# Dynamic convolution with a gated two-stage network: row-half streams from the second head on, eight unsplit experts in the second stage, no join, every task's place written out

## The chip, the cores and the metric

The kernel runs on one core of a Trainium2 chip. A core has TensorE (PE in the rows; PEld is its weight load), VectorE (DVE), ScalarE (ACT), GpSimd (POOL) and SyncE (SP, which here only issues DMAs). They run at the same time, each through its own instructions in order, and wait for each other by semaphores. The metric is the device time of one execution in microseconds (us). TensorE's granted clock was 1.000 over the whole span, the upper of its two levels.

## The reference, cut to what matters

```python
# stage 1: x (4, 4160, 192), weight_gen (4, 4160, 8, 7)
w = softmax(weight_gen, axis=-1)                    # 7 taps for each token and head
out[b, s, h, g] = sum_k w[b, s, h, k] * x_pad[b, s + k, h, g]     # 6 zeros ahead of x
# stage 2: w_in (192, 1024), conv_w (3, 1024), w_out (1024, 192)
h = maximum(out @ w_in, 0)
conv = sum_k conv_w[k] * h_pad[:, k:k + S]          # over 3 neighbouring tokens
y = (h * sigmoid(conv)) @ w_out                     # (4, 4160, 192), float32
```

## The kernel before, in words

The 16,640 tokens lie on 128 partitions, 130 on each. A block `j` is 4 of these (512 tokens); there are 33 blocks. The 1024 hidden columns are 8 groups of 128, which the change's title calls experts (`f`). The work of a block is:

- **Head** `q`: POOL multiplies x by seven taps into `px` and `py` (for the first two heads VectorE takes some). For heads 0 to 2 TensorE sums the seven products while it transposes them; from head 3 on two accumulating DMAs and two POOL adds sum them first, so that only 6 transposes are left. ScalarE (`split_hi`) and VectorE (`split_lo`) write the transposed tile as a rounded part and a rest: `H1` and `L1` for the first 128 columns of x, `H2` for the last 64, with the rounded part in rows 0 to 63 and the rest in rows 64 to 127.
- **First stage**, `unit(j, f)`: matmuls of `wi` with `H1`, `H2`, `L1` into one of five PSUM banks `z`; ScalarE writes `relu` into `h` and the middle tap of the convolution back into `z`; VectorE adds the two side taps (`conv_side`, two instructions); ScalarE takes the tanh; VectorE multiplies (`gmul`). A DMA carries the last two rows of `h` to the next block.
- **Second stage**, `out_tiles(j)`: four output tiles of 128 tokens (two in block 0), each the sum over the 8 groups of `g` (stationary) times `wo` (192 columns, moving) in one of two PSUM banks, which ScalarE evicts to `o`; a DMA stores `o`.

TensorE can work in two **streams**: matmuls on rows 0 to 63 and on rows 64 to 127 run beside each other. The planner calls them `P0` and `P8`, and `P` where both are held by a matmul of 128 rows. Both halves of a sum go into the same bank, so the second half of a unit or tile waits until the first has ended (`leads`). Both streams share one queue of instructions.

Before the change the first stage runs in streams from block 7 on (`HALF`), the heads' transposes from head 8 (`HALF_T`), the output tiles in blocks 5 to 30 (`HALF_O`). In full rows a unit is 5 matmuls of 512 columns; in streams it is 9 half ones, since the rest of `H2` isn't needed against the small part of the weights. A DMA copies the rounded half of `H2` to the other rows (`HB`), so that each stream can take the odd matmul in some units.

In blocks 2 to 31 the groups 0 and 1 (`NS = 2`) are **split**: after `gmul`, ScalarE rounds `g` into `gx` (`g_hi`, L509) and VectorE writes the rest (`g_lo`, L512). `wo` is split alike (`wos`). A split group costs a tile one matmul of 384 columns and one of 192 in the faster float32r form; an unsplit one is one float32 matmul of 192 columns, which the trace shows as two records. The 384 columns leave a second partial sum, so ScalarE evicts 384 columns (L574) and POOL adds the halves (`join`, L580) before the store.

The order on each engine comes from a planner with a table of durations. Its first 700 tasks are listed by number (`ORDER`) and come first; all others follow by a list schedule improved by one pass backwards and forwards (`greedy`, `place`, `ROUNDS`).

Of the kernel before, what the change touches and what calls it, by code (L numbers as in the profile page):

```python
# [17 lines left out]
P = 128  # L18
# [28 lines left out]
LAST = 1  # L47
HALF = 7
HALF_T = 8
HALF_O = 5  # L50
CHUNKS = 4
TWIN = (3, 4, 5, 6)
# [53 lines left out]
def kernel(  # L106
# [32 lines left out]
    gx_p = ctx.enter_context(tc.tile_pool(name="gx", bufs=2))  # L139
    o_p = ctx.enter_context(tc.tile_pool(name="o", bufs=2))  # L140
# [10 lines left out]
    NP = NF - NS  # L151
    wo = const.tile([P, NF, D], F32, name="wo")
    wos = const.tile([P, NS, 2, D], F32R, name="wos")
# [8 lines left out]
    t_b = [[const.tile([P, W], F32R, name=f"{t}_{i}") for t in ("H1", "L1", "H2")] for i in range(2)]  # L162
    twin_b = const.tile([P, W], F32R, name="HB")
# [232 lines left out]
    def turn(q, part, c, s, dst):  # L396

        r = slice(s * H2_, (s + 1) * H2_)
        src = px_b[q % NX][r, 2].rearrange("p s d -> p (s d)")
        n = R2 if part else R  # L400
        return nc.tensor.matmul(  # L401
            dst[:, c * P + s * H2_:c * P + (s + 1) * H2_], lhsT=src[:, (part * R + c) * P:(part * R + c + 1) * P], rhs=ident[r, r],
            is_transpose=True, start=(s == 0 and c == 0), stop=(s == 1 and c == n - 1), skip_group_check=True,
        )
# [27 lines left out]
    z_t, g_t, gs_t, gx_t = {}, {}, {}, {}  # L432
# [8 lines left out]
    def mm1(j, f):  # L441
        z = z_t[j, f] = z_b[z_ix(j * NF + (f if j else FORD.index(f)))]
        fs = slice(f * P, (f + 1) * P)
        terms = [(wh[:, 0], "H1"), (wl[:, 0], "H1"), (wh[:, 1], "H2"), (wl[:, 1], "H2"), (wh[:, 0], "L1")]
        for i, (w, nm) in enumerate(terms):
            nc.tensor.matmul(out=z, lhsT=w[:, fs], rhs=h_t[j, nm], start=(i == 0), stop=(i == len(terms) - 1))  # L446

    def mm1_half(j, f, s):

        if not s:  # L450
            z_t[j, f] = z_b[z_ix(j * NF + f)]
# [3 lines left out]
        if s == (f in TWIN):  # L455
            terms.insert(3, (wl[r, 1], "HB" if s else "H2"))
# [31 lines left out]
    def halves(j):  # L488
        return FIRST <= j < NB - LAST

    def split(j, f):
        return f < NS and halves(j)

    def gx_of(j, f, b):
        if j not in gx_t:
            gx_t[j] = gx_p.tile([P, NS, 2, W], F32R if halves(j) else F32, tag="gx", name="gx")
        return gx_t[j][:, f, b, :geom(j)[0] * P]

    def g_of(j, f):
        if split(j, f):  # L500
            return z_t[j, f]
        if f < NS:
            return gx_of(j, f, 0)
        if j not in g_t:
            g_t[j] = g_p.tile([P, NP, W], F32, tag="g", name="g")
        return g_t[j][:, f - NS, :geom(j)[0] * P]

    def g_hi(j, f):
        nc.scalar.activation(out=gx_of(j, f, 0), in_=g_of(j, f), func=ACTF.Copy)  # L509
# [670 lines left out]
```

## Time and profile before

| what | value |
|---|---|
| three runs | 709.66, 710.46, 712.53 us; median 710.46 |
| the profiled execution: its own time | 709.04 us |
| its span, first to last instruction | 707.3 us |
| outside its span | 1.74 us |
| TensorE busy | 685.6 us (97%) |
| VectorE, ScalarE, POOL busy | 653.3, 596.7, 567.3 us (92, 84, 80%) |

An engine counts as busy while at least one of its instructions is in flight. Matmuls overlap each other, and with two streams one stream can stand still while the other keeps the engine "busy". So TensorE's 97% isn't the share of time in which it is fed; that has to be worked out from counts and intervals.

### The profile page before, as it was taken

How to read it: one execution, taken by the hardware profiler on the slowest of the kernel's cores; microseconds unless marked ns; L12 is line 12 of the kernel's file. 1: busy time of each engine (PE TensorE's matmuls, PEld its weight loads, DVE VectorE, ACT ScalarE, POOL GpSimd, SP SyncE). 2: the span in 40 equal slices, each digit the busy share in tenths (PEclk: the TensorE clock that was granted, in tenths of full speed). 3: DMA queues.
4: the chain of work that ended last, by engine and by line, in shares of the span. 5: the costliest groups of instructions: out<-in, count | busy, mean ns of one | idle time of the engine just before them, and what ended most of it. 6: DMA issues, size and time to landing. Idle time of an engine off the chain costs nothing.

```text
span 707.3 us, 16723 instructions
## 1 busy us (share of the span) xinstructions
PE 685.6 (97%) x6395; PEld 646.7 (91%) x6395; DVE 653.3 (92%) x1058; ACT 596.7 (84%) x1149; POOL 567.3 (80%) x448
## 2 busy tenths in 40 slices
PE   4899999999999999999999999999999999999997
PEld 4788889888889999999999999999999999999987
DVE  7999999997799999999999999989999999899981
ACT  4789899878788988888899889979899888888881
POOL 6999999979899799999886998879898897812111
PEclk9999999999999999999999999999999999999999
DMA  8739899987897979699868897798978879672201
GB/s 219 254 110 220 210 191 215 231 191 180 201 217 189 218 150 240 173 238 226 201 179 202 172 243 179 185 241 195 235 176 202 209 143 212 161 174 85 81 38 45
DMA packets 56505, 131.37 MB, mean 186 GB/s; under 512 B 5471, under 2 KB 10206, under 8 KB 56425
## 3 DMA queue, kind: packets, MB, share of 16 engines
q0 software_dynamic: 20192, 59.01, 47.1%
q1 hardware_dynamic: 35914, 70.84, 29.4%
q8 instruction: 50, 0.82, 0.5%
q10 hardware_dynamic: 318, 0.46, 0.3%
q14 instruction: 31, 0.25, 0.1%
HBM read 20.51 MB, written 12.78 MB: 47 GB/s over the span
## 4 chain that ended last, share of the span: by engine, by line
PE 74%; DVE 9%; POOL 5%; DMA 4%; ACT 3%; issue 3%; SPq 0%; DVEq 0%; POOLq 0%; ACTq 0%
PE ops L565 35%; PE z L457 31%; DVE z L479 4%; PE ops L555 4%; PE z L446 2%; DMA h<-h 2%; DMA px<-py 2%; POOL py L349 2%; DVE g L524 1%; POOL px L349 1%; PE tp L401 1%; ACT h L468 1%; DMA stage<-in_moe_w_in_dram 1%; PE z L555 1%; ACT z L472 1%
## 5 line engine op out<-in xcount | busy, mean ns | idle before, releaser
L479 DVE SCALAR_TENSOR_TENSOR z<-h,cw,z 128x512 f32<-128x512 f32 (+1 forms) x528 | 374.7, 740 | 18.0 <-ACT z L472 14.5
L565 PE MATMUL ops<-wo,g 64*128 64x192 f32 x2496 | 348.2, 325 | 0.0
L457 PE MATMUL z<-H,wi 64*128 64x512 f32 x1352 | 328.4, 414 | 2.1 <-DVE gx L512 1.8
L565 PEld LDWEIGHTS ops<-wo,g 64*128 64x128 f32 x2496 | 313.3, 187 | 0.9
L349 POOL TENSOR_TENSOR px<-ring,w 128x768 f32<-128x768 f32 (+1 forms) x145 | 235.0, 1901 | 6.5 <-PE tp L401 4.8
L457 PEld LDWEIGHTS z<-H,wi 64*128 64x128 f32 x1352 | 208.1, 185 | 10.6 <-DVE gx L512 2.7
L472 ACT ACTIVATE z<-h,cw 128x512 f32<-128x512 f32 (+1 forms) x264 | 179.6, 686 | 4.3
L486 ACT ACTIVATE z<-z 128x512 f32<-128x512 f32 (+1 forms) x264 | 150.8, 576 | 38.2 <-DVE z L479 36.6
L349 POOL TENSOR_TENSOR py<-ring,w 128x768 f32<-128x768 f32 (+3 forms) x108 | 171.3, 1878 | 0.0
L468 ACT ACTIVATE h<-z 128x512 f32<-128x512 f32 x264 | 155.7, 596 | 17.6 <-PE z L457 9.5
L457 PE MATMUL z<-L,wi 64*128 64x512 f32 x416 | 147.3, 392 | 0.0
L524 DVE SCALAR_TENSOR_TENSOR g<-z,h 128x512 f32<-128x512 f32 (+1 forms) x198 | 132.7, 677 | 6.1 <-ACT z L486 4.4
L565 PE MATMUL ops<-wos,gx 64*128 64x384 f32 (+1 forms) x832 | 133.4, 312 | 2.4 <-ACT o L574 2.4
L580 POOL TENSOR_TENSOR o<-o 128x768 f32<-128x768 f32 x30 | 68.2, 2274 | 72.4 <-ACT o L574 57.3
L565 PEld LDWEIGHTS ops<-wos,gx 64*128 64x128 f32 x832 | 107.7, 186 | 9.6 <-ACT o L574 4.1
L375 POOL TENSOR_TENSOR px<-px 128x512 f32<-128x512 f32 (+1 forms) x60 | 71.6, 1425 | 4.4 <-DMA px<-px 4.4
L457 PEld LDWEIGHTS z<-L,wi 64*128 64x128 f32 x416 | 72.8, 184 | 1.9
L574 ACT ACTIVATE o<-ops 128x384 f32<-128x384 f32 (+1 forms) x128 | 60.9, 478 | 16.2 <-PE ops L555 7.9
L446 PE MATMUL z<-H,wi 128*128 128x512 f32 x224 | 64.8, 410 | 1.6 <-DVE g L524 0.9
L368 POOL DMA_DIRECT2D px<-px x30 | 40.0, 1332 | 26.5 <-DMA px<-py 26.3
L555 PE MATMUL ops<-wo,g 128*128 128x192 f32 x288 | 51.1, 327 | 0.0
L446 PEld LDWEIGHTS z<-H,wi 128*128 128x128 f32 x224 | 39.9, 188 | 12.0 <-DVE g L524 2.6
(91 smaller groups left out, 704.0 us busy)
## 6 DMA issues: line engine op xcount, KB each, us to landing
px<-py POOLq DMA_DIRECT2D x30, 1152.0 KB, 10.3
h<-h SPq DMA_DIRECT2D x128, 256.0 KB, 4.7
px<-px POOLq DMA_DIRECT2D x30, 768.0 KB, 7.3
ring<-in_x_dram SPq DMA_DIRECT2D x31, 384.0 KB, 5.3
out_dram<-o SPq DMA_DIRECT2D x31, 384.0 KB, 6.8
w<-in_weight_gen_dram SPq DMA_DIRECT2D x15, 224.0 KB, 2.9
HB<-H SPq DMA_DIRECT2D x26, 128.0 KB, 4.8
r_out<-in_moe_w_out_dram SPq DMA_DIRECT2D x4, 384.0 KB, 5.8
```

The source lines that it names most:

```text
L349: eng.tensor_tensor(out=dst[:, a:b, :].rearrange("p s (h g) -> p s h g", g=GRP), in0=ring[:, p:p + n, :].rearrange("p s (h g) -> p s h g", ...
L375: nc.gpsimd.tensor_tensor(out=dst.rearrange("p (s d) -> p s d", s=R), in0=a[:, :, lo:hi], in1=b[:, :, lo:hi], op=ALU.add)
L446: nc.tensor.matmul(out=z, lhsT=w[:, fs], rhs=h_t[j, nm], start=(i == 0), stop=(i == len(terms) - 1))
L457: return [lambda i=i, w=w, nm=nm: nc.tensor.matmul(out=z, lhsT=w[:, fs], rhs=h_t[j, nm][r], start=(not s and i == 0), stop=(s == 1 and i = ...
L468: nc.scalar.activation(out=hrow(f, 2, R), in_=rows(z_t[j, f]), func=ACTF.Relu)
L472: nc.scalar.activation(out=rows(z_t[j, f][:, :no * P]), in_=hrow(f, cc, no), func=ACTF.Copy, scale=cw[:, NF + f:NF + f + 1])
L479: nc.vector.scalar_tensor_tensor(out=z, in0=hrow(f, cc + d, no), scalar=cw[:, k * NF + f:k * NF + f + 1], in1=z, op0=ALU.mult, op1=ALU.add,)
L486: nc.scalar.activation(out=z, in_=z, func=ACTF.Tanh, scale=0.5)
L524: nc.vector.scalar_tensor_tensor(out=rows(g_of(j, f)), in0=rows(z_t[j, f][:, :no * P]), scalar=1.0, in1=hrow(f, cc, no), op0=ALU.add, op1= ...
L555: nc.tensor.matmul(out=ps[:, 0:m], lhsT=g, rhs=w, start=(n == 0), stop=(n == len(terms) - 1))
L565: return nc.tensor.matmul(out=hold[0][2][:, 0:m], lhsT=g[r], rhs=w[r], start=(not s and n == 0), stop=(s == 1 and last), skip_group_check= ...
L580: eng.tensor_tensor(out=o[:, 0, a:b], in0=o[:, 0, a:b], in1=o[:, 1, a:b], op=ALU.add)
```

## The change

The streams now begin with head 1 and block 0 and last to block 31; only head 0's transposes and the last block's output tiles use 128 rows (`FULL_T`, `FULL_O`). `HB` is made for every head and has two buffers; units 4 to 7 of a block use it. The heads 1 and 2, which sum seven products, are transposed in streams too, the narrow part as 64 by 64 pieces.

The split is gone: `g_hi`, `g_lo`, `wos`, `gx`, the second partial sum and `join`. All 8 groups of `g` lie in one tile of SBUF with two buffers. An eviction has 192 columns everywhere. An output tile's task is cut in four pieces of two groups, and each waits for its own groups, not for all eight. `o` has four buffers of half the size, and an eviction waits for the store four blocks back, not two.

`ORDER` has all 4,766 tasks; `greedy`, `place` and the passes are gone.

```diff
-HALF = 7
-HALF_T = 8
-HALF_O = 5
+FULL_T = 1
+FULL_O = 1
-TWIN = (3, 4, 5, 6)
+TWIN = 4
...
-    "344 7 8 9 10 11 12 13 14 25 27 28 29 133 26 30 34 31 32 134 141 142 135 144 36 37 136 146 16 17 38 35 39 40 18 "
+    "0 1 2 6 15 24 33 44 53 64 3 4 5 392 393 7 8 9 10 11 12 13 14 25 26 27 131 28 132 133 34 135 35 134 148 138 149 "
...
-    o_p = ctx.enter_context(tc.tile_pool(name="o", bufs=2))
+    o_p = ctx.enter_context(tc.tile_pool(name="o", bufs=4))
...
+    def late(j, f):
+        return (f if j else FORD.index(f)) >= TWIN
...
-        if s == (f in TWIN):
+        if s == late(j, f):
             terms.insert(3, (wl[r, 1], "HB" if s else "H2"))
...
-    def g_hi(j, f):
-        nc.scalar.activation(out=gx_of(j, f, 0), in_=g_of(j, f), func=ACTF.Copy)
-
-    def g_lo(j, f):
-        (nc.vector if GL[f] == "V" else nc.gpsimd).tensor_tensor(
-            out=gx_of(j, f, 1), in0=g_of(j, f), in1=gx_of(j, f, 0).bitcast(F32), op=ALU.subtract
-        )
...
+    def mm2(j, i, s, first, last, n, hold):
+        if first and n == 0:
+            hold[0] = (j, i, hold[0] or out_bank(i))
+        c, r = slice(i * P, (i + 1) * P), slice(0, P) if s is None else slice(s * H2_, (s + 1) * H2_)
+        return nc.tensor.matmul(
+            out=hold[0][2][:, 0:D], lhsT=g_of(j, n)[r, c], rhs=wo[r, n, :], start=(first and n == 0), stop=(last and n == NF - 1),
+            skip_group_check=True)
...
-        n = 2 if halves(j) else 1
-        nc.scalar.activation(
-            out=o_t[j][:, 0:n, i, :], in_=ps[:, 0:n * D].rearrange("p (b d) -> p b d", b=n), func=ACTF.Copy, scale=0.5
-        )
-
-    def join(eng, j, a, b):
-        o = o_t[j]
-        eng.tensor_tensor(out=o[:, 0, a:b], in0=o[:, 0, a:b], in1=o[:, 1, a:b], op=ALU.add)
+        nc.scalar.activation(out=o_t[j][:, i, :], in_=ps[:, 0:D], func=ACTF.Copy, scale=0.5)
...
+            k_ = 4 if late(j, f) else 5
+            a_ = task("P0", 0.231 * k_, deps_, (k_, lambda: mm1(j, f, 0)), after=[last_mm[0]] + ([] if n else zfirst))
+            mm[n] = task("P8", 0.231 * (9 - k_), [a_] + (twins[j] if late(j, f) else []), (9 - k_, lambda: mm1(j, f, 1)),
+                         after=[last_mm[1]])
...
+                            + ([] if k else [gm[j * NF + f] for f in ns]),
...
-        head_ = [num[int(a)] for a in ORDER.split()]
-        taken = set(head_)
-        rest = [i for i in sorted(range(nt), key=lambda i: (best[i], pos[i])) if i not in taken]
-        seq = [i for i in head_ + rest if tasks[i][3] is not None]
+        order = [int(a) for a in ORDER.split()] or list(range(nt))
+        assert sorted(order) == list(range(nt))
```

**How the order moves.** First TensorE at the start of block 0, before the change. `tp` and `ops` are PSUM banks that the heads are transposed into, `px0` and `px1` the products of heads 0 and 1, `z1` to `z3` the banks of the first three units; a shape of 128x512 is a unit's matmul.

```order
L392 MATMUL ops_180<-ident_79,px0_99 64x128 x4
L392 MATMUL tp_175<-ident_79,px0_99 128x128 x4
L392 MATMUL ops_287<-ident_79,px1_100 64x128 x4
L446 MATMUL z1_112<-H1_0_104,wi_82 128x512 x2
L446 MATMUL z1_112<-H2_0_106,wi_82 128x512 x2
L446 MATMUL z1_112<-L1_0_105,wi_82 128x512
L392 MATMUL tp_309<-ident_79,px1_100 128x128 x8
L392 MATMUL ops_287<-ident_79,px1_100 64x128 x8
L446 MATMUL z2_113<-H1_0_104,wi_82 128x512 x2
```

The same place after the change:

```order
L563 MATMUL tp_208<-ident_76,px0_95 128x128 x4
L574 MATMUL tp_284<-ident_76,px1_96 128x64
L574 MATMUL ops_286<-ident_76,px1_96 64x64
L574 MATMUL tp_284<-ident_76,px1_96 128x64
L574 MATMUL ops_286<-ident_76,px1_96 64x64
L574 MATMUL tp_284<-ident_76,px1_96 128x64
L574 MATMUL ops_286<-ident_76,px1_96 64x64
L574 MATMUL tp_284<-ident_76,px1_96 128x64
L574 MATMUL ops_286<-ident_76,px1_96 64x64
L625 MATMUL z1_109<-H1_0_100,wi_79 128x512 x2
L625 MATMUL z1_109<-H2_0_102,wi_79 128x512 x2
```

Head 1's transposes, in runs of 4 and 8 of 128 rows before, are now half ones that alternate between pieces of 128x64 (`tp`, one stream) and 64x64 (`ops`, the other). Over the whole program 170 neighbouring pairs of matmuls change between a piece of 64x64 and one of 64 rows by 128 columns.

Next TensorE in the steady part, where an output tile ends and the next one in the same bank begins. Before (`ops_5871` and `ops_5999` share a bank, `ops_5950` has the other):

```order
L565 MATMUL ops_5871<-wo_83,g_5640 128x192
L565 MATMUL ops_5950<-wo_83,g_5640 128x192
L565 MATMUL ops_5871<-wo_83,g_5640 128x192
L457 MATMUL z4_115<-H1_0_104,wi_82 128x512 x2
L457 MATMUL z4_115<-H2_0_106,wi_82 128x512
L457 MATMUL z4_115<-L1_0_105,wi_82 128x512
L565 MATMUL ops_5999<-wos_84,gx_5571 128x384
L565 MATMUL ops_5999<-wos_84,gx_5571 128x192
```

After the change (`ops_4005` and `ops_4122` share a bank):

```order
L682 MATMUL ops_4005<-wo_80,g_3806 128x192
L625 MATMUL z0_108<-L1_0_101,wi_79 128x512
L682 MATMUL ops_4069<-wo_80,g_3806 128x192
L625 MATMUL z4_112<-H1_0_100,wi_79 128x512 x2
L682 MATMUL ops_4069<-wo_80,g_3806 128x192
L625 MATMUL z4_112<-H2_0_102,wi_79 128x512
L625 MATMUL z0_108<-H1_0_100,wi_79 128x512
L625 MATMUL z4_112<-L1_0_101,wi_79 128x512
L625 MATMUL z0_108<-H1_0_100,wi_79 128x512
L682 MATMUL ops_4122<-wo_80,g_3806 128x192
```

Before, the four matmuls of `z4` between the two tiles all lie in the other stream, so nothing covers the eviction of `ops_5871` in the stream that `ops_5999` starts on. After, five half matmuls of units (the one of `z0` from `L1` and the four of `z4`) lie in that stream between `ops_4005` and `ops_4122`.

Last, ScalarE in the steady part. Before (L574 is an eviction, L509 the rounding of `g`):

```order
L486 ACTIVATE z2_113<-z2_113 128x512
L574 ACTIVATE o_3738<-ops_3819 128x2x192
L509 ACTIVATE gx_3940<-z2_113 128x512
L486 ACTIVATE z3_114<-z3_114 128x512
L468 ACTIVATE h_85<-z4_115 128x4x128
L472 ACTIVATE z4_115<-h_85,cw_81 128x512
L486 ACTIVATE z0_111<-z0_111 128x512
L509 ACTIVATE gx_3940<-z3_114 128x512
```

After (L689 is the eviction):

```order
L640 ACTIVATE z2_110<-h_81,cw_78 128x512
L598 ACTIVATE H1_0_100<-tp_4163 128x512
L689 ACTIVATE o_4111<-ops_4122 128x192
L654 ACTIVATE z1_109<-z1_109 128x512
L636 ACTIVATE h_81<-z3_111 128x4x128
L654 ACTIVATE z2_110<-z2_110 128x512
L640 ACTIVATE z3_111<-h_81,cw_78 128x512
```

The roundings of `g` are gone, and an eviction of 192 columns stands between the instructions of the first stage, about one to every two units.

## Rows read from the trace of the kernel before

**Rows 1.** The page: its first line.
```profile
span 707.3 us, 16723 instructions
```

**Rows 2.** Windows, all engines: stretch, length, busy us and count of each engine.
```profile
39.60:118.10 78.50, 77.64 (x426) 68.41 (x425) 78.04 (x132) 69.62 (x136) 78.11 (x64) 1.00 0.83 196
118.10:207.80 89.70, 85.62 (x708) 76.95 (x708) 80.00 (x128) 73.84 (x141) 80.38 (x66) 1.00 0.88 202
207.80:648.10 440.30, 439.43 (x4649) 425.68 (x4647) 420.75 (x662) 389.52 (x739) 370.25 (x287) 1.00 0.83 195
```

**Rows 3.** Windows of L446, full-row unit matmuls (PE busy, count, then PEld).
```profile
0.00:39.60 39.60, 11.18 (x40) 7.06 (x41) 1.00 0.74 220
...
39.60:118.10 78.50, 41.91 (x161) 28.96 (x162) 1.00 0.83 196
```

**Rows 4.** The same windows of L392, the full-row transposes.
```profile
0.00:39.60 39.60, 17.82 (x132) 16.25 (x132) 1.00 0.74 220
...
39.60:118.10 78.50, 7.79 (x57) 6.51 (x55) 1.00 0.83 196
```

**Rows 5.** Window of L555, the records of full-row output tiles.
```profile
39.60:118.10 78.50, 35.22 (x208) 33.52 (x208) 1.00 0.83 196
```

**Rows 6.** Windows of L457 and of L565: half matmuls of units, of tiles.
```profile
207.80:648.10 440.30, 328.58 (x1585) 236.55 (x1585) 1.00 0.83 195
...
207.80:648.10 440.30, 358.64 (x2800) 330.60 (x2798) 1.00 0.83 195
```

**Rows 7.** Timeline, PE, full rows: start us, us, instruction.
```profile
15.15 1.04 PE L392 MATMUL ops<-ident,py 128*64 128x128 f32 x8
16.02 1.04 PE L392 MATMUL tp<-ident,py 128*128 128x128 f32 x8
...
24.64 1.08 PE L446 MATMUL z<-H,wi 128*128 128x512 f32 x4
25.56 0.39 PE L446 MATMUL z<-L,wi 128*128 128x512 f32 x1
...
105.22 0.72 PE L555 MATMUL ops<-wos,gx 128*128 128x384 f32 x4
...
107.74 0.60 PE L392 MATMUL tp<-ident,px 128*128 128x128 f32 x4
...
692.83 0.81 PE L555 MATMUL z<-wo,gx 128*128 128x192 f32 x4
...
700.63 0.81 PE L555 MATMUL ops<-wo,gx 128*128 128x192 f32 x4
```

**Rows 8.** Timeline, PE, half rows.
```profile
299.56 0.40 PE L401 MATMUL tp<-ident,px 64*128 64x64 f32 x4
...
410.13 0.40 PE L457 MATMUL z<-H,wi 64*128 64x512 f32 x1
...
410.60 0.40 PE L457 MATMUL z<-H,wi 64*128 64x512 f32 x1
```

**Rows 9.** Timeline, PE and ACT, where an output bank turns over.
```profile
485.69 0.99 PE L565 MATMUL ops<-wo,g 64*128 64x192 f32 x10
...
487.29 0.58 PE L565 MATMUL ops<-wos,gx 64*128 64x384 f32 x4
...
486.74 0.49 ACT L574 ACTIVATE o<-ops 128x384 f32<-128x384 f32 x1
```

**Rows 10.** Timeline, PE, where full rows change to half rows.
```profile
150.60 0.39 PE L446 MATMUL z<-L,wi 128*128 128x512 f32 x1
150.92 0.82 PE L565 MATMUL ops<-wos,gx 64*128 64x384 f32 x8
```

**Rows 11.** Groups by line, DVE: the subtraction that the split needs.
```profile
L512 DVE TENSOR_TENSOR gx<-z,gx 128x512 fp32r<-128x512 f32 x60 | 40.8, 684 | 1.6 <-ACT gx L509 1.4
```

**Rows 12.** Waits of PE, from 150 to 646 us.
```profile
PE z L457 <- DMA HB<-H: 0.4, 1, 0.4
```

**Rows 13.** Timeline: the last eviction.
```profile
703.43 0.33 ACT L574 ACTIVATE o<-ops 128x192 f32<-128x192 f32 x1 [2.27 <-PE ops L555]
```

More of the change, by code (lines that the diff above doesn't have):

```diff
@@ L439, in z_ix, with mm1 @@
         return (1 + n) % 4 if n < NF else (4, 1, 2, 3, 0)[(n - NF) % NZ]
[L441 to L448, printed above, removed]
+    def late(j, f):
+        return (f if j else FORD.index(f)) >= TWIN
+    def mm1(j, f, s):
         if not s:
-            z_t[j, f] = z_b[z_ix(j * NF + f)]
+            z_t[j, f] = z_b[z_ix(j * NF + (f if j else FORD.index(f)))]
         z = z_t[j, f]
@@ L558, in mm2_half @@
-    def mm2_half(j, i, s, hold):
-        def one(n, last):
-            if not s and n == 0:
-                hold[0] = (j, i, out_bank(i))
-            m, g, w = mm2_terms(j, i)[n]
-            r = slice(s * H2_, (s + 1) * H2_)
-            return nc.tensor.matmul(
-                out=hold[0][2][:, 0:m], lhsT=g[r], rhs=w[r], start=(not s and n == 0), stop=(s == 1 and last), skip_group_check=True)
-        k = NF + (NS if halves(j) else 0)
-        return [(0.327 if n >= 2 * NS or not halves(j) else (0.118, 0.172)[(n + 1) % 2], lambda n=n: one(n, n == k - 1)) for n in range(k)]
+    def mm2(j, i, s, first, last, n, hold):
[5 more added lines that the diff above has]
+            skip_group_check=True)
@@ new lines, in head, with one, whole @@
+            hd = [mm_end[q - 2][0], mm_end[q - 2][1]] if q >= 2 else []
+            xend, yend, ends_ = [], [], [None, None]
+            for part in (0, 1):
+                b_ = part if multi else 0
+                pr = part == 1 and not multi
+                nc_ = R2 if pr else R
+                def one(n, c, s, part=part, b_=b_, lead=part if multi else 0, nc_=nc_):
+                    if n == 0 and c == 0 and s in (None, lead):
+                        hold[part] = (ps_o if b_ else ps_t).tile(
+                            [P, W], F32, tag="ops" if b_ else "tp", name="ops" if b_ else "tp")
+                    i, end = out_[n][0], n == len(out_) - 1 and c == nc_ - 1
+                    return turn(q, i, part, c, s, hold[part], n == 0 and c == 0 and s == lead, end and s == 1 - lead)
+                def whole(n, part=part, b_=b_):
+                    if n == 0:
+                        hold[part] = (ps_o if b_ else ps_t).tile(
+                            [P, W], F32, tag="ops" if b_ else "tp", name="ops" if b_ else "tp")
+                    return transposes(q, out_[n][0], part, hold[part], n == 0, n == len(out_) - 1)
+                f_ = None
+                for s in (None,) if q < FULL_T else (part if multi else 0, 1 - part if multi else 1):
+                    for n, (i, e_) in enumerate(out_):
+                        after = [f_] if n or s == (1 - part if multi else 1) else bank[b_]
+                        if s is None:
+                            f_ = task("P", 0.11 * nc_, [e_] + after, [(0.11 * nc_, lambda n=n, whole=whole: whole(n))])
+                        else:
+                            f_ = task("P8" if s else "P0", 0.06 * nc_, [e_] + after,
+                                      [(0.06, lambda n=n, c=c, s=s, one=one: one(n, c, s)) for c in range(nc_)])
+                        (xend if i < 4 else yend).append(f_)
+                a_ = task("A", 0.56 if pr else 0.49, [f_] + hd, lambda part=part, pr=pr: split_hi(q, part, hold[part], pr))
+                l_ = task("V", 0.78 if pr else 0.6, [a_], lambda part=part, pr=pr: split_lo(q, part, hold[part], pr))
+                spl_done.setdefault(q, []).append(l_)
+                if part:
+                    twins[q] = [task("none", 2.2, [task("H", 0.4, [a_] + hd, lambda: twin(q))])]
+                bank[b_] = [l_]
@@ L969, in out_tiles @@
-                e_ = task("A", act(D * (1 + hv)) + 0.02, [a_] + (stored[-2:][:1] if i == 0 and len(stored) > 1 else []),
+                hold = {0: None}
+                if z_:
+                    hold[0] = z_b[z_ix(NU + i // 2)]
+                deps_ = wo_rdy + ([mm[NU - 1], (zl + zfree)[-NZ]] if z_ else bank[1 + i % 2])
+                full = j >= NB - FULL_O
+                a_ = None
+                for k, s in enumerate((None,) if full else (0, 1)):
+                    for c in range(CHUNKS):
+                        ns = range(NF * c // CHUNKS, NF * (c + 1) // CHUNKS)
+                        a_ = task(
+                            "P" if full else ("P0", "P8")[s], 0.326 * len(ns), (deps_ if not k and not c else []) + ([a_] if k else [])
+                            + ([] if k else [gm[j * NF + f] for f in ns]),
+                            [(0.326, lambda n=n, s=s, k=k, hold=hold, i=i: mm2(j, i, s, k == 0, full or k == 1, n, hold)) for n in ns],
+                            after=[a_ if c else ends.get(s)])
+                    ends[s] = a_
@@ L970, in out_tiles @@
+                tiles[j, i] = a_
+                e_ = task("A", act(D) + 0.02, [a_] + (stored[-4:][:1] if i == 0 and len(stored) > 3 else []),
                           lambda hold=hold: evac(*hold[0]), begun=last_evac)
@@ L986, in attention @@
             head(q)
-        now[0] = FIRST - 1.5
-        ws_rdy = w_split()
         attention(0)
@@ L1096 @@
+        seq = [i for i in sorted(range(nt), key=lambda i: (best[i], pos[i])) if tasks[i][3] is not None]
         told, asks, last = {}, {}, None
@@ L1124 @@
         steps.sort(key=lambda x: x[:2])
-        leads = {}
-        for i in range(nt):
-            if eng[i] == "P8":
-                ps_ = [d for d, _ in preds[i] if eng[d] == "P0"]
-                if ps_:
-                    leads[i] = max(ps_)
+        leads = {i: max(ps_) for i in range(nt) if eng[i] in ("P0", "P8")
+                 for ps_ in [[d for d, _ in preds[i] if eng[d] in ("P0", "P8") and eng[d] != eng[i]]] if ps_}
         lead_end = {d: None for d in leads.values()}
```

258 lines of the change are left out of this document (31 added, 227 removed), and 230 rows, old and new, of the table ORDER.

## Prediction

> **What bounds the kernel now.** I read the windows by stage first, then the counts of TensorE's matmuls in them, then single stretches of the timeline for the interval from one matmul to the next, and last the waits. In the windows [rows 2] TensorE counts as busy nearly all the time, but with two streams that says little: one stream can stand while the other is in flight. What TensorE has to do is found as count times interval.
>
> The intervals. Four unit matmuls of full rows start in 0.92 us, 0.23 each [rows 7]; in one stream two intervals take 0.47 us [rows 8]; I use 0.232 us for both. Three unsplit tiles take 7.80 us from start to start, 2.60 each; a split tile's 4 and 12 records take 2.52 us [rows 7]. A full-row transpose takes 0.109 us (eight in 0.87), a half one 0.06: four last 0.40, of which one alone takes 0.22 [rows 7, 8]. A tile in two streams takes each stream as long as a tile in full rows takes the engine, since a half matmul still has all its columns.
>
> Now three stretches, with TensorE's work in each.
> - 0 to 39.6 us: 40 unit matmuls and 132 transposes [rows 3, 4], 9.3 + 14.4 = 23.7 us. Idle 15.9 us: the start, before data and weights are there.
> - 39.6 to 118.1 us, blocks 1 to 4: 161 unit matmuls, 57 transposes, 208 tile records, which are 13 tiles, 6 of them unsplit [rows 3 to 5]: 37.4 + 6.2 + 6 x 2.60 + 7 x 2.52 = 76.8 of 78.5 us. Idle 1.7 us, 0.43 a block. VectorE is busy for 78.04 us [rows 2]: both engines are full. The listed order covers this stretch.
> - 207.8 to 648.1 us, 22 blocks (1585 half matmuls, 72 a block) [rows 6]: per stream 792 x 0.232 = 183.9, 2800 / 32 = 87.5 tiles x 2.52 = 220.5, and by the code 132 half transposes, 7.9; 412 of 440.3 us. Idle 28 us, 1.27 a block. VectorE is busy 420.75 us, 96% [rows 2]. Here the list schedule set the order.
>
> Over the whole program the work, with the counts by the code, is 280 full-row and 936 half matmuls per stream, 282.1 us; 10 unsplit and 120 split tiles, 328.4; 198 full and 150 half transposes, 30.6; together 641.1 us of the span of 707.3 [rows 1]. Of the 66.2 us of idle stream, 15.9 are the start, 1.7 blocks 1 to 4, 3.9 the time after the last tile [rows 13], and 44.7 the 28 blocks from 5 to 32: 1.60 a block, more than in the long stretch, because between 118.1 and 207.8 us both TensorE and VectorE stand (85.62 and 80.00 of 89.7 busy) [rows 2]. That is where the list ends. So TensorE's work bounds the kernel, with VectorE close behind, and about 45 us go to stalls that the two give each other and that the order makes.
>
> **The change, part by part.**
>
> Streams in the units of blocks 0 to 6: 56 units lose half a matmul of 0.232 us, 6.5 us. Head transposes: 56 full ones (head 0), then per stream 112 (heads 1 and 2) and 180 (30 heads of 6): 6.1 + 17.5 = 23.6 us, 7.0 less.
>
> No split: 120 tiles go from 2.52 to 2.60 us, 9.6 us more. TensorE's new work is 275.6 (1188 x 0.232) + 338.0 (130 x 2.60) + 23.6 = 637.2 us, 3.9 us less than before. So the change of arithmetic by itself is worth next to nothing on TensorE; the time lies in the idle 66 us.
>
> What the split's end frees lies elsewhere. VectorE loses two of L512 a block; in all 40.8 us [rows 11], 1.36 a block. In the long stretch its 420.75 us become 420.75 - 30 = 391, 17.8 a block, against TensorE's 8.35 + 10.40 + 0.36 = 19.1. Before, VectorE had 19.1 a block and TensorE 18.7 of work: one always waited for the other. Now one leads by 1.3 us a block. ScalarE loses two roundings a block and a third of each eviction (0.49 to 0.33 us) [rows 9, 13]; POOL loses the join, and the stores that waited for it start earlier. I cost these at nothing: they aren't on the path, they loosen it.
>
> Start and blocks 1 to 4: set by VectorE too. It loses two L512 in each of blocks 2 to 4, 6 x 0.684 = 4.1 us [rows 11]; TensorE loses 16 matmuls and head transposes, about as much. Both shrink together, so I keep the idle 1.7 us, and the start's 15.9, since its loads, decoding and taps are the same.
>
> More `HB` copies, 33 for 26, on SP's queue; in front of TensorE's queue, now for units 4 to 7 of every block. Behind a unit that waits stands all of TensorE. One such wait is in the trace, 0.4 us [rows 12], with one buffer; there are two now. Nothing; at the other end 0.4 us at each of 33 heads, 13 us.
>
> The tile turnover. Before, with no cover in its stream, the next tile began 0.61 us after the last record of the old one ended (486.68 to 487.29), 0.49 of it the eviction [rows 9]. With 0.33 us it is 0.45; the last record is in flight for 0.16 us after its slot (four take 0.81 us, three intervals of 0.163 and the last one's 0.32) [rows 7], so 0.61 us of stream time are needed. The order after has five half matmuls there, 1.16 us: 0.55 us to spare. Covered, if ScalarE is no later than that.
>
> Stalls of the 28 blocks from 5 on, not shown for this order: the bounds are 0 and the 1.60 a block of now; rows lie at 0.43 (listed order, full rows) and 1.27 (list schedule, streams). I take 0.55, near the first: the whole order is listed, output tiles alternate with units rather than come in bunches, and the second-fullest engine has 7% to spare, which it hadn't at 0.43 either. 28 x 0.55 = 15.4 us.
>
> Sum: 637.2 + 15.9 + 1.7 + 3.9 + 15.4 = 674.1 us of span; with the 1.74 us that lie outside it, 675.8 us. The profiled execution (709.04) is 0.2% under the runs' median, so I say 677 us, 4.7% less.
>
> Changes of shape in the array: 170 in heads 1 and 2, from 64 by 128 to 64 by 64 and back. In the trace a change of rows costs 0.09 us (0.32 instead of 0.23 from the last matmul of full rows to the first half ones) [rows 10]; a change of columns alone, 128 to 64 and back, costs nothing (the eight transposes before the change at 16.02 take 0.87 us, as 8 x 0.109) [rows 7]. The new changes are of columns alone, so I take 0 by the nearest row; the other end is 170 x 0.09 = 15.3 us. The Trainium skill speaks against it: "TensorEngine Tiling (Array Packing)", Key Properties, says that changing the tiling mode, not just the tile, drains TensorE. The trace agrees for rows and not for columns; by that rule the sum would be 691 us.
>
> **The rivals.**
> - *The streams themselves stall* (1.27 to 1.6 a block stay). For it: the stretch with 1.27 is the one in streams, and one queue feeds both, so a matmul that waits holds up the other stream. Against: the stalls there also meet a VectorE that is 96% busy. Price: 20 to 29 us more, 696 to 706 us.
> - *Each change of shape drains*: 170 x 0.09, while VectorE covers little: 685 to 692 us.
> - *Slower: the tile turnover.* 126 tiles wait for an eviction with 0.55 us to spare. If ScalarE is held by VectorE's side taps when an eviction is due, each late 0.5 us costs up to 63 us: 739 us. It decides from 0.30 us a tile, 38 us, where the sum passes 714. Against it: ScalarE loses about a tenth of its work.
> - *No gain*: VectorE's order, and not its load, sets the pace; the 1.6 us a block stay and the copies of `HB` cost 5: 707 to 714.
>
> **How the numbers follow.** A measurement of this kernel can tell about 0.5%, 3.6 us, from no change: faster is under 706.9, slower over 714. The forecast (662 to 690) has 0.62, streams that stall 0.17, drains 0.09, no gain 0.05, slower 0.07. Faster: 0.62 + 0.09 + 0.15 of the streams' 0.17 = 0.86; same 0.07 (the rest of the streams' case and no gain); slower 0.07. The range goes from almost no stall (none gives 658.7 + 1.7 = 660.4) to stalls of 1.4 a block and a median that lies 1.4 us over the profiled time (658.7 + 39.2 + 1.7 + 1.4 = 701.0): 662 to 702; the forecast's own is 662 to 690.
>
> **What would show it.** Right: VectorE busy about 610 us; in the middle the blocks come every 19.5 to 19.8 us (72 half matmuls of units each) instead of 20.0; the stretch after block 4 has no dip on both engines. Wrong: TensorE waiting for L689 in many tiles (turnover); intervals of 0.15 us among the half transposes of heads 1 and 2 (drains); blocks still 20 us apart with VectorE under 90% busy (streams).

## The result and the profile after

The changed kernel takes 693.31 us (median of four runs, 691.93 to 695.77); the kernel before, run beside it, 710.91. The ratio is 0.9755, with a 95% interval of 0.972 to 0.979: faster by 17.6 us, where the forecast was 34. A second measurement further below gives 693.41 us and 0.9745 [0.9723, 0.9768]. The time lies in the forecast range (662 to 702) but outside the likeliest case's own range (662 to 690). The profiled execution took 691.93 us.

The page, first line and busy times (against [rows 1]), and then the windows of [rows 2] on the kernel after:

```profile
span 690.1 us, 17906 instructions
PE 665.9 (96%) x7113; PEld 649.5 (94%) x7113; DVE 625.2 (91%) x998; ACT 558.7 (81%) x1088; POOL 513.9 (74%) x417
```

```profile
core 0: us, PE busy (x) PEld busy (x) DVE busy (x) ACT busy (x) POOL busy (x), PEclk, DMA share, GB/s
39.60:118.10 78.50, 73.84 (x780) 68.56 (x778) 73.06 (x126) 64.21 (x126) 75.66 (x62) 0.98 0.85 201
118.10:207.80 89.70, 89.70 (x986) 89.36 (x984) 84.51 (x130) 77.41 (x149) 79.98 (x65) 1.00 0.97 224
207.80:648.10 440.30, 438.38 (x4801) 434.17 (x4799) 413.82 (x642) 374.46 (x721) 327.78 (x263) 1.00 0.83 195
```

The dip between 118.1 and 207.8 us is gone: TensorE is busy for 89.70 us of it (85.62 before). The first stretch, which was full before, now has 73.84 of 78.5 us, and its clock is 0.98. The middle is best read by blocks. The next row is the window of L625, the half matmuls of the units, over ten blocks (72 a block; the 721st only touches the window).

```profile
456.90:649.50 192.60, 171.13 (x721) 120.30 (x722) 1.00 0.74 176
```

A block takes 19.26 us there, where 1585 matmuls in 440.3 us made 20.0 before [rows 6]. TensorE's work in a block is 19.1 us by the prediction's sum, so the stall is 0.2 us a block, not the 0.55 of the forecast. Yet the sum missed by 16 us. I divided the whole trace as the prediction does: a block begins with the first matmul of its first unit, the work of a stream is count times interval (0.231, 0.1625, 0.061 and 0.109 us), and what is left is idle stream.

| stretch | idle, forecast | idle, after |
|---|---|---|
| up to block 1 (starts at 45.3 us, 39.6 before) | 15.9 | 25.7 |
| blocks 1 to 4 (to 127.7 us) | 1.7 | 9.9, of it 5.4 in block 4 |
| blocks 5 to 31 | 14.9 | 9.1, of it 4.2 in block 13 |
| block 32 to the end | 4.4 | 9.0 |
| sum | 36.9 | 53.7 |

With 636.3 us of work the right column gives the span of 690.1 us to 0.1 us. (The forecast's 15.4 us are spread at 0.55 a block.) The two streams don't pass from one block to the next at the same time. Counting all matmuls that start in a stretch, over both streams, the four numbers are 26.3, 11.3, 9.2 and 7.0 us. Either way most of the error lies in the first 128 us.

Block 4, in the timeline of the kernel after (start, us, instruction, in brackets the idle time before it and what ended it), four engines:

```profile
104.92 0.33 SPq L416 DMA_DIRECT2D w<-in_weight_gen_dram  x1
108.03 0.69 DVE L663 SCALAR_TENSOR_TENSOR g<-z,h 128x512 f32<-128x512 f32 x1
112.61 0.62 DVE L456 TENSOR_REDUCE m<-w 128x64 f32<-128x448 f32 x1 [3.89 <-DMA w<-in_weight_gen_dram]
113.93 0.58 ACT L654 ACTIVATE z<-z 128x512 f32<-128x512 f32 x1 [4.48 <-DVE z L647]
114.42 0.33 ACT L689 ACTIVATE o<-ops 128x192 f32<-128x192 f32 x1
111.59 0.32 PE L682 MATMUL ops<-wo,g 64*128 64x192 f32 x1
114.80 0.43 PE L682 MATMUL ops<-wo,g 64*128 64x192 f32 x1 [2.88 <-ACT o L689]
116.12 0.79 PE L625 MATMUL z<-L,wi 64*128 64x512 f32 x1
```

VectorE reaches the maximum of softmax group 7, whose weights were only requested at 104.92, and stands 3.89 us for them. Behind it stand the side taps, behind these ScalarE's tanh, behind that an eviction, and behind the eviction TensorE, 2.88 us. Then the matmuls are slow for a while (0.79 us in flight at 116.12, 0.39 otherwise). The granted clock of the stretch 114.8 to 119.0 us is 0.59. In block 13 it is an exponential of group 10 on ScalarE, which waits 3.20 us for a late POOL step; the next eviction and TensorE stand behind it:

```profile
288.95 0.58 ACT L462 ACTIVATE w<-w 128x448 f32<-128x448 f32 x1 [3.20 <-POOL w L459]
292.28 0.31 ACT L689 ACTIVATE o<-ops 128x192 f32<-128x192 f32 x1
292.65 0.55 PE L682 MATMUL ops<-wo,g 64*128 64x192 f32 x1 [1.92 <-ACT o L689]
```

The start, in windows of the kernel after:

```profile
20.00:26.50 6.50, 4.33 (x48) 2.96 (x43) 4.79 (x12) 2.49 (x6) 6.04 (x6) 1.00 0.70 185
26.50:33.50 7.00, 6.49 (x30) 4.76 (x30) 5.51 (x12) 3.74 (x8) 6.41 (x5) 0.51 0.86 269
```

TensorE is busy for 4.33 of 6.5 us, and then its clock is granted at 0.51 for 7 us, the lower of its two levels; in the profiled execution of the kernel before it was 1.00 throughout.

### The profile page after: what moved, and what is told of

Same layout as the page of the kernel before. It is cut to its first block, busy times and chain, and to the rows that moved or that the text cites. A ratio compares the mean times of both kernels' runs of the same rounds, so it can differ in the third digit from the quotient of the medians.

```text
span 690.1 us, 17906 instructions
## 1 busy us (share of the span) xinstructions
PE 665.9 (96%) x7113; PEld 649.5 (94%) x7113; DVE 625.2 (91%) x998; ACT 558.7 (81%) x1088; POOL 513.9 (74%) x417
## 4 chain that ended last, share of the span: by engine, by line
PE 71%; POOL 16%; DMA 9%; issue 1%; ACT 1%; DVE 1%; SPq 1%; POOLq 0%; DVEq 0%
PE ops L682 37%; PE z L625 32%; POOL px L520 6%; POOL py L520 6%; DMA px<-py 5%; DMA ring<-in_x_dram 2%; DMA w<-in_weight_gen_dram 2%; PE tp L574 1%; POOL px L539 1%; POOL px L546 1%; PE z L682 1%; POOL w L481 1%; POOL px L536 1%; POOL w L459 1%; DVE z L647 0%
## 5 line engine op out<-in xcount | busy, mean ns | idle before, releaser
L682 PE MATMUL ops<-wo,g 64*128 64x192 f32 (+1 forms) x4064 | 575.8, 326 | 5.3 <-ACT o L689 4.8
L682 PEld LDWEIGHTS ops<-wo,g 64*128 64x128 f32 (+1 forms) x4064 | 543.8, 188 | 9.4 <-ACT o L689 5.5
L625 PE MATMUL z<-H,wi 64*128 64x512 f32 x1716 | 470.5, 425 | 2.2 <-DVE g L663 1.1
L625 PEld LDWEIGHTS z<-H,wi 64*128 64x128 f32 x1716 | 288.7, 187 | 6.8 <-PE z L625 1.5
L625 PE MATMUL z<-L,wi 64*128 64x512 f32 x528 | 203.8, 394 | 0.0
L663 DVE SCALAR_TENSOR_TENSOR g<-z,h 128x512 f32<-128x512 f32 (+1 forms) x264 | 178.1, 679 | 6.7 <-ACT z L654 3.7
L520 POOL TENSOR_TENSOR py<-ring,w 128x768 f32<-128x768 f32 (+2 forms) x108 | 168.0, 1841 | 0.0
L625 PEld LDWEIGHTS z<-L,wi 64*128 64x128 f32 x528 | 97.1, 186 | 1.0
L689 ACT ACTIVATE o<-ops 128x192 f32<-128x192 f32 x128 | 41.7, 326 | 15.6 <-PE ops L682 14.1
L625 PE MATMUL z<-HB,wi 64*128 64x512 f32 x132 | 52.1, 395 | 0.0
L574 PE MATMUL tp<-ident,px 64*128 64x64 f32 x424 | 47.6, 223 | 1.8 <-DVE L L602 1.7
L574 PEld LDWEIGHTS tp<-ident,px 64*128 64x128 f32 x424 | 45.1, 139 | 4.3 <-POOL px L520 1.9
```

The source lines that it names most:

```text
L520: eng.tensor_tensor(out=dst[:, a:b, :].rearrange("p s (h g) -> p s h g", g=GRP), in0=ring[:, p:p + n, :].rearrange("p s (h g) -> p s h g", ...
L574: return nc.tensor.matmul(dst[0:D2 if part and i >= 0 else P, c * P + s * H2_:c * P + (s + 1) * H2_], lhsT=src, rhs=ident[r, r], is_transp ...
L625: return [lambda i=i, w=w, nm=nm: nc.tensor.matmul(out=z, lhsT=w[:, fs], rhs=h_t[j, nm][r], start=(not s and i == 0), stop=(s == 1 and i = ...
L663: nc.vector.scalar_tensor_tensor(out=rows(g_of(j, f)), in0=rows(z_t[j, f][:, :no * P]), scalar=1.0, in1=hrow(f, cc, no), op0=ALU.add, op1= ...
L682: return nc.tensor.matmul(out=hold[0][2][:, 0:D], lhsT=g_of(j, n)[r, c], rhs=wo[r, n, :], start=(first and n == 0), stop=(last and n == NF ...
```

## The experiments

The theory after the result: the mechanism in the middle is right, and the loss sits in a few instructions that stand too early in an in-order engine's queue, and at the start in the clock. The rivals: TensorE's own turnover and streams; or POOL, which would take back whatever is freed. A table of what was found, with block starts and idle stream worked out as above ("20 to 31" is per block). Medians and ratios come from 4 to 10 executions, the other columns from the single one that was profiled, which can lie up to 4.5 us from the median:

| kernel | median us | ratio to before, 95% | block 1 at | block 5 at | idle in block 4 | idle in block 13 | 20 to 31 |
|---|---|---|---|---|---|---|---|
| after | 693.31 | 0.9755 [0.972, 0.979] | 45.3 | 127.7 | 5.4 | 4.2 | 0.20 |
| after, again | 693.41 | 0.9745 [0.9723, 0.9768] | 45.5 | 129.7 | 7.2 | 4.3 | 0.21 |
| later maximum | 695.40 | 0.9757 [0.9715, 0.9799] | 47.1 | 124.5 | 0.4 | 8.7 | 0.20 |
| and exponential | 688.02 | 0.9660 [0.9617, 0.9703] | 46.7 | 124.1 | 0.4 | 0.3 | 0.20 |
| full-row heads | 699.20 | 0.9810 [0.9774, 0.9847] | 50.1 | 132.0 | 4.0 | 4.1 | 0.20 |
| filler | 694.24 | 0.9751 [0.9706, 0.9797] | 43.5 | 129.1 | 7.3 | 2.2 | 0.19 |
| all softmax later | 690.71 | 0.9707 [0.9677, 0.9738] | 47.2 | 124.6 | 0.4 | 0.3 | 0.20 |
| and filler | 690.72 | 0.9711 [0.9668, 0.9754] | 46.0 | 124.4 | 0.4 | 0.3 | 0.20 |
| after, list schedule | 717.89 | 1.0088 [1.0056, 1.012] | 47.9 | 127.2 | 0.9 | 1.4 | 1.27 |
| before, list schedule | 714.36 | 1.0049 [1.0026, 1.0073] | | | | | |
| VectorE load back | 705.22 | 0.9909 [0.989, 0.9929] | 45.4 | 130.5 | 7.2 | 2.4 | 0.77 |
| second copy | 697.78 | 0.9820 [0.9794, 0.9845] | 44.8 | 129.0 | 7.0 | 4.7 | 0.38 |
| softmax and loads | 687.81 | 0.9674 [0.9637, 0.9711] | 45.0 | 124.1 | 2.1 | 0.3 | 0.20 |

### One maximum later

```diff
 order = [int(a) for a in ORDER.split()] ...
+for a, b in ((1775, 854),):
+    order.remove(a)
+    order.insert(order.index(b), a)
```

> One VectorE instruction moved: the maximum of softmax group 7 (L456), which waited 3.89 us for its load in block 4 and held every side tap behind it, stands some 19 us later in the order, still 15 us ahead of its reader. If that one wait made the loss at block 4 (5.4 us of idle stream there, the stretch of half clock after it included), the time falls from 693.3 to about 688 (687 to 689.5), block 5 starts at about 122.5 instead of 127.7 us and everything after it is as much earlier. If the loss is TensorE's own (the tile turnover or the streams), or if the next late thing takes the wait's place (POOL stood 0.76 us for a fold's DMA just there), the time stays at 692 to 694.

Task 1775 is the maximum, now ahead of task 854. Block 4 behaves as expected: its idle stream falls to 0.4 us, block 5 starts at 124.5 us. But the time does not move: of the 3.2 us that block 5 is earlier, 0.5 are left at block 13, and block 14 starts 3.9 us later than in the kernel after. This kernel's timeline, ScalarE, POOL and TensorE in block 13:

```profile
284.64 0.60 ACT L654 ACTIVATE z<-z 128x512 f32<-128x512 f32 x1
292.46 0.58 ACT L462 ACTIVATE w<-w 128x448 f32<-128x448 f32 x1 [7.23 <-POOL w L459]
290.99 1.44 POOL L459 TENSOR_TENSOR w<-w,m 128x448 f32<-128x448 f32 x1
296.15 0.68 PE L682 MATMUL ops<-wo,g 64*128 64x192 f32 x1 [5.93 <-ACT o L689]
```

The exponential's wait grew from 3.20 to 7.23 us: ScalarE was free 0.5 us earlier, and POOL's step came 3.5 us later (at 290.99 us; 287.49 in the kernel after). Why POOL's step was later stays open. So the first stall was real and the rival was right about the time: the next wait took it.

### And one exponential later

```diff
-for a, b in ((1775, 854),):
+for a, b in ((1775, 854), (2626, 2024), (2627, 2031), (2628, 2081)):
```

> The same, and also the exponential, the sum and the small addition of softmax group 10 about 10 us later in the order (ScalarE waited 3.20 us there for a POOL step that was itself late, in block 13, with an eviction behind it). If that wait made the 4.2 us of idle stream in block 13, the time is 4 us under that of the kernel with the first move alone: about 684 (682.5 to 685.5), and every block from 5 to 31 then takes 19.1 to 19.4 us. If TensorE would have stood there anyway, it is equal to that kernel within 1 us.

Block 13's stall is gone (0.3 us), and the ratio falls to 0.966. The time is 688.02 us, not the 684 expected. The two waits together are worth about 6 us; small ones of 1.0 to 2.4 us stand in blocks 8, 10 and 16.

### Heads 1 and 2 in full rows

```diff
 f_ = task("P8" if s else "P0", 0.06 * nc_, [e_] + after,
-          [(0.06, lambda ...: one(n, c, s)) for c in range(nc_)])
+          ([(0.06 * nc_, lambda ...: whole(n))] if s == (part if multi else 0) else None)
+          if q < FULL_T + 2 else [(0.06, lambda ...: one(n, c, s)) for c in range(nc_)])
```

> The changed kernel with the transposes of heads 1 and 2 in full rows again, at the places of the first half; nothing else moved. Each head then costs TensorE 2.7 us more (56 x 0.109 against 56 x 0.061). If the start is set by VectorE, POOL and the weights, this is nearly free: block 1 at 45 to 46 us, 692 to 695. If it is the changes of shape in the halves that cost (0.09 us each) or the idle that they leave and the half clock after it (26.3 to 33.8 us), the granted clock stays 1.00, block 1 starts 2 to 4 us earlier and the time is 689 to 691. If TensorE's own work sets the start, it is 5 us slower: 698.

The clock stays at 1.00 in this execution, with TensorE busy for 6.31 of the 6.5 us from 20.0 and for all of the next 7. Yet block 1 starts at 50.1 us, 4.8 us later, and the ratio is 0.981: the third case of the expectation. So the half transposes pay in the start, nearly by the 5.4 us that they save, and they show no cost at the changes of shape. The timeline of the kernel after shows that too, both shapes beside each other, each about 0.06 us after the last of its own:

```profile
34.06 0.22 PE L574 MATMUL tp<-ident,px 64*128 64x64 f32 x1
34.09 0.22 PE L574 MATMUL ops<-ident,px 64*64 64x64 f32 x1
34.13 0.22 PE L574 MATMUL tp<-ident,px 64*128 64x64 f32 x1
34.15 0.22 PE L574 MATMUL ops<-ident,px 64*64 64x64 f32 x1
34.19 0.22 PE L574 MATMUL tp<-ident,px 64*128 64x64 f32 x1
```

### Filler for the clock

```diff
+filler = {(172, 0): 1, (173, 0): 4, (213, 0): 2, (213, 1): 1, (190, 0): 2}
 for _, k, e, i, fn in steps:
+    for _ in range(filler.get((i, done.get(i, 0)), 0)):
+        nc.tensor.matmul(z_b[0], lhsT=wh[:, 0, 0:P], rhs=h_t[0, "H1"], start=True, stop=True, ...)
...
```

> Ten matmuls of full rows by 512 columns, whose result is overwritten, are put into TensorE's waits between 23.0 and 27.9 us of the start, 2.3 us in 2.5 us of waits; nothing else moved. If the clock falls to 0.50 at 26.3 us because TensorE stood there, and the half clock costs what it seems to (matmuls at 0.43 to 0.46 us for 7.5 us), the clock stays at 1.00, block 1 starts at 42 to 43 us instead of 45.3 and the time is 690 to 691. If the waits for VectorE, ScalarE and POOL set the start and the clock only follows, the clock stays up but block 1 starts at 44.5 to 45.5 us: 692.5 to 693.5. If the clock doesn't answer to the filler, the time is 693 to 694.

The windows of this kernel, as those of the kernel after above:

```profile
20.00:26.50 6.50, 6.18 (x57) 4.44 (x57) 5.26 (x14) 2.84 (x8) 6.50 (x6) 1.00 0.63 167
26.50:33.50 7.00, 7.00 (x87) 5.29 (x89) 6.51 (x13) 5.07 (x12) 6.45 (x5) 1.00 0.89 276
```

With TensorE kept busy the clock stays at 1.00 here, and the half clock has a price: block 1 starts at 43.5 us, and at 44.8 to 47.2 us in the kernels of the same start without filler. That is 1.3 to 3.7 us of the start's extra 9.8. At block 5 nothing of it is left (129.1 us; 127.7 and 129.7 in the two executions of the changed kernel), with 7.3 us of idle in block 4, against 5.4 and 7.2. This execution is also the fastest of the filler's four: 691.10 us with a mean clock of 0.998 over the span, the others 694.08 to 697.69 us with 0.985 to 0.990, as without filler. With the softmax steps moved too (next), the half clock came earlier in that execution, ahead of the filler (0.57 to 0.50 from 22 to 28 us), so the filler isn't a sure remedy.

### All softmax steps later, without and with filler

```diff
+for a, b in ((1775, 854), (1494, 770), (1495, 779), (1496, 852), ..., (4326, 3737)):
```

> The maximum of softmax group 7 as before, and for every group from 6 on ScalarE's exponential placed at least 11 us behind the POOL step that it reads, with the sum and the small addition behind it; group 10 is one of them. With the maximum and group 10 alone, 4 waits of ScalarE for POOL (5.5 us) were left, and TensorE stood at tiles 0.5 to 1.0 us at 195.9, 226.0, 236.6 and 348.9 us; blocks 8, 10 and 16 had 1.0, 2.35 and 1.5 us of idle stream. If these come from the exponentials too, each block from 5 on has 0.1 to 0.5 us, and the ratio to before is 0.960 to 0.963 (4 us under 0.966). If POOL's folds, waiting for their DMA (61 us in 25 waits), hold the heads anyway, the stalls move to other places and the ratio stays at 0.966.

> The same and the ten filler matmuls at the start. With the filler alone the granted clock stayed up and block 1 came at 43.5 us instead of 45.3 to 47.1, but the gain was used up at block 4, where the wait for the load grew from 5.4 to 7.3 us. If that load's wait was what took it, with the maximum out of the way 2 to 3.5 us of it arrive at the end: ratio 0.956 to 0.960, block 5 at 120.5 to 121.5 us. If POOL's taps set the pace up to block 5 (POOL is busy for 90 to 100 per cent of 30 to 110 us), block 5 comes at 123 to 124 us as without the filler, and the two kernels of this pair are equal within 1 us.

Without filler blocks 5 to 17 now have 0.07 to 0.45 us of idle each, as expected, but one stall of 1.6 us in block 18 remains (with filler 1.6 us in block 16 and 2.7 in block 18), and the ratio is no better than with two moves. In the five kernels that have the later maximum block 5 starts at 124.1 to 124.6 us, for a block 1 anywhere from 45.0 to 47.2 us: within that range something other than TensorE sets the pace up to there. POOL is the candidate, because it is busy for 75.66 of the 78.5 us from 39.6 on. Its folds' waits for their DMA, 52 us in 20 waits in the kernel after, are not the reason, since only 2.5 us of them lie before 128 us. That POOL sets it is argued, not shown.

### The order taken out, with either structure

```diff
-order = [int(a) for a in ORDER.split()]
+cur = greedy(rank) ...
```

> The changed kernel's structure (streams from the second head on, eight unsplit experts, no join) with the written order taken out and the list scheduler of the kernel before in its place. Beside it runs the kernel before with its own listed order taken out. If the gain comes from the structure (VectorE loses 1.36 us a block), this one is near the changed kernel in the middle: blocks of 19.4 to 19.8 us, and 690 to 698 in all. If the written order carries it, blocks stay at 19.8 to 20.2 us and the time is 705 to 715, near that of the kernel before.

> The kernel before without its listed order for the first blocks, so that its list scheduler sets everything: the pair of the run above, structure apart. Its middle (207.8 to 648.1 us) was made by the scheduler already and should take 20.0 us a block as it did; only the start can be slower, 712 to 722.

Here `greedy` and the passes are those of the kernel before. This is the main finding. Under the same list scheduler the new structure is not faster than the old but 0.5% slower, 717.89 against 714.36 us. The written order is worth 24.5 us on the new structure; no run has the old structure with an order written throughout. The loss per block is 1.27 us, as it was before the change; and no wait for VectorE shows in it: VectorE is busy for 286.27 us (89%) of the 320 from 320 to 640, while TensorE counts as busy all the time and, outside the start, waits 0.7 us in all for evictions. The timeline of this kernel shows where it is (L476 are tiles, L419 units, L368 transposes):

```profile
564.00 0.34 PE L368 MATMUL tp<-ident,px 64*128 64x64 f32 x3
564.14 0.32 PE L476 MATMUL ops<-wo,g 64*128 64x192 f32 x1
564.18 0.22 PE L368 MATMUL tp<-ident,px 64*128 64x64 f32 x1
564.30 0.83 PE L476 MATMUL ops<-wo,g 64*128 64x192 f32 x4
564.97 0.40 PE L368 MATMUL tp<-ident,px 64*128 64x64 f32 x4
565.21 0.38 PE L476 MATMUL ops<-wo,g 64*128 64x192 f32 x1
565.34 0.47 PE L419 MATMUL z<-H,wi 64*128 64x512 f32 x1
```

The first four transposes end one stream's work (rows 0 to 63, by the code). From 564.24 us on the queue holds four tile records, four transposes and another record, all of the other stream, 0.163 and 0.06 us apart. The next unit of rows 0 to 63 stands behind them and starts at 565.34: 1.1 us in which half of the array has nothing, and no view counts it as idle. Nine of the ten blocks from 451 to 655 us have this hole, 1.1 us in the mean, most of that stream's 1.27; the other stream loses as much at other places.

### VectorE's load put back

```diff
 nc.vector.scalar_tensor_tensor(out=rows(g_of(j, f)), in0=rows(z_t[j, f]...), ...)
+if 2 <= j < NB - 1 and f % 4 == 0:
+    nc.vector.scalar_tensor_tensor(out=rows(scr[0]...), in0=rows(z_t[j, f]...), ...)
```

> The changed kernel with the VectorE load of the split put back: behind two of the eight gate products of each of 30 blocks VectorE does the product once more, into a scratch tile (2 x 0.68 us a block, as the two L512 of before, reading the same bank of z; the result is not used). If the order alone made the gain and VectorE's relief is not needed for it, blocks stay at 19.2 to 19.5 us, because VectorE has 1.1 us a block to spare, and the time is at most 5 us above the changed kernel's. If the relief is what lets the streams run, VectorE's 18.1 us a block become 19.5, the blocks take 19.7 to 20.2 us and the time is 705 to 715.

11.8 us more than the changed kernel beside it, so the relief is needed. Waits of TensorE's weight load for evictions over the whole span, and of ScalarE's tanh for the side taps from 320 to 640 us, first in this kernel (L693 is the eviction there), then in the kernel after (us in total, times, longest):

```profile
PEld ops L686 <- ACT o L693: 17.9, 33, 3.9
ACT z L654 <- DVE z L647: 40.4, 69, 1.3
```

```profile
PEld ops L682 <- ACT o L689: 5.5, 2, 3.2
ACT z L654 <- DVE z L647: 10.0, 25, 1.0
```

These waits are those of the prediction's slower rival: VectorE late, ScalarE held by its side taps, evictions late, tiles waiting for a bank. The window from 320 to 640 us has VectorE at 311.58 of 320 us in this kernel and at 302.51 in the kernel after. At blocks of 19.9 us the former is 19.3 us of VectorE's work a block, more than TensorE's 19.1, so VectorE may also set the pace simply as the fullest engine. This run doesn't tell the two apart.

### Each eviction twice

```diff
+nc.scalar.activation(out=scr[0]..., in_=ps[:, 0:D], func=ACTF.Copy, scale=0.5)
 nc.scalar.activation(out=o_t[j][:, i, :], in_=ps[:, 0:D], func=ACTF.Copy, scale=0.5)
```

> The changed kernel with each eviction done twice, first into a scratch tile: ScalarE is held 0.21 to 0.33 us longer before the bank of an output tile is free, 130 times (27 to 43 us more on an engine that is busy for 559). The prediction's slower case was that tiles wait for their banks, with 0.55 us to spare. If the cover is as it was worked out, 692 to 697; if the turnover is on the edge, each tile is 0.2 to 0.3 us late and the time is 715 to 730.

4.4 us more, just above the range of the first case: 0.03 us a tile for an eviction that is 0.2 to 0.3 us later. Loads of weights do wait for evictions here, nearly as often as with VectorE's load put back:

```profile
PEld ops L682 <- ACT o L690: 13.3, 26, 4.1
```

Idle stream in blocks 20 to 31 is 0.38 us a block, against 0.20. So the bank's turnover is covered for the most part, and the number of such waits doesn't give their cost.

### Loads at the start in another order, with the later softmax steps

```diff
+for a, b in ((81, 924), (924, 99), (511, 99), (1775, 854), ..., (4326, 3737)):
```

> The later softmax steps, and at the start three loads in another order on SP's queue: the weights of softmax group 2 first (VectorE and POOL wait 0.5 us each for them at 24 us), those of group 4 and the rows of head 4 behind the second spread of the input weights and the load of group 3, since nothing reads them before 30 and 46 us. If the loads' order makes a part of the start's loss, block 1 starts at 43 to 45 us instead of 45.3 to 47.2 and the time is 1 to 3 us under that with the softmax steps alone (ratio 0.966 to 0.970). If POOL and VectorE set the first 125 us, block 5 still comes at 124 to 125 us and the ratio is as it was, 0.966 to 0.971.

> The changed kernel itself on the same chip and beside the same runs, as the measure for the three others: ratio 0.972 to 0.979 as at first.

Block 1 starts at 45.0 us, which the kernels with the old order of loads reach too (44.8 to 47.2), and block 5 at 124.1: no effect of the loads' order is shown. With 687.81 us this kernel is 5.6 us under the changed one beside it, ratio 0.9674 against 0.9745 with intervals that don't meet. From the kernel with two moves alone (0.9660) and that with all softmax steps later (0.9707) it can't be told apart.

## Why the prediction was right and wrong

**Right: the arithmetic of TensorE.** 1188 x 0.231, 130 x 16 x 0.1625, 56 x 0.109 and 292 x 0.061 us make 636.3 us, forecast 637.2.

**Right: no cost for the changes of shape.** The transposes of heads 1 and 2 start 0.06 us apart, not 0.15. The rule of the Trainium skill, "TensorEngine Tiling (Array Packing)", Key Properties, that a change of tiling mode drains TensorE, is not borne out by this trace for 64 by 128 against 64 by 64, which run beside each other. The trace shows the shapes of the matmuls; whether the array's mode changes between these two it does not show.

**Right: `HB` at nothing.** None of TensorE's waits in the trace after is for `HB`.

**Right with a condition: the turnover.** Two tiles of 130 wait for an eviction (4.8 us), both behind an instruction that had nothing to do with tiles. The doubled eviction cost 4.4 us, with 26 loads of weights that waited. With VectorE's old load 33 wait, and the time is 11.8 us longer. So the five half matmuls cover an eviction that is 0.2 to 0.3 us later, and whether they cover more depends on VectorE's margin.

**Wrong: "I keep the idle 1.7 us, and the start's 15.9".** This is the step that failed: 25.7 and 9.9 us came out, 18.0 more, against an error of 16.8 in the sum of idle time, and so the gain is 17.6 us and not 34. The argument was that both engines lose about as much work there, so that idle time stays as it was. Of the start's 9.8 us the half clock made 1.3 to 3.7, by one execution with filler. Full-row transposes or other loads did not bring the rest back, and what sets it stays open. In blocks 1 to 4 a maximum placed ahead of its weights made 5.0 of the 5.4 us in block 4 (0.4 are left with the maximum later), which no term of the sum had: there it was the place of an instruction, not the amount of work. The other 3.2 us that these blocks lost beyond the forecast stay open.

**Right in its total, wrong in its kind: the stalls.** 15.4 us at 0.55 a block were forecast for blocks 5 to 32. From block 5 on idle stream is 18.1 us with the tail, forecast 19.3. That they agree is luck: a normal block has 0.2 us, one wait of ScalarE in block 13 makes 4.2, and the last stretch has 9.0 against 4.4.

**Wrong: the cause of the 1.27 us a block.** The prediction put them down to two engines of which "one always waited for the other", and made VectorE's relief the reason why they would shrink. With the relief and the list schedule they stay, 1.27 us a block, as holes in one stream; that was the rival of streams that stall. With the order and without the relief they are 0.77, with both 0.20. So it needs both: the order closes the holes of the one queue, and VectorE's margin lets the order hold. That the kernel before lost its 1.27 us a block in the same way does not follow from the same size, and the two traces don't look alike. From 0.3 us before the first to 0.6 us after the last of each run of half transposes lie 17.5 of 26.1 us of idle stream in the new structure with the list schedule (220 to 650 us), but 8.6 of 28.3 us in the kernel before (208 to 648 us), each in a fifth of the time. So what made the loss of the kernel before stays open. VectorE was busy for 625 us, not about 610, and ScalarE for 559, 6% less and not a tenth.

## What to carry to other kernels

An order written out is a set of promises about latencies. In an in-order engine look for instructions whose reader is far off and whose input comes from the slowest part (a load, a POOL step), and place them late: one maximum that nobody read for another 30 us and one exponential that could stand 10 us later cost about 6 us together, and mending the maximum alone left a longer wait at the exponential. When two streams share a queue, the busy share hides a stream that stands, so count matmuls and intervals per block. And a gain of structure and order together can't be split by argument: each has to be taken out alone.

## What was not expected of the hardware

TensorE's granted clock fell to about 0.5 after a stretch in which it was busy for 4.33 of 6.5 us, its longest wait there 1.04 us, and again after single waits of 2.88 us (0.59 from 114.8 to 119.0) and 1.92 us (0.57 from 292.6 to 296.6). With ten matmuls in those waits at the start it stayed at 1.00 in one execution. How long the half clock lasts at the start differs between executions of the same beginning: from 33.5 to 45 us it is 1.00 in the kernel changed again, where block 1 comes at 45.5 us, and 0.82 in the kernel with one maximum later, where it comes at 47.1. Over all of them block 1 comes between 44.8 and 47.2 us; that is as large as several of the effects looked for here.
